# A long convolution with two expert layers: the filter's second layer in two passes, with its stored half reloaded in place

## The chip, the cores and the metric

The program runs on one core of a Trainium2 chip. The core has five engines that work side by side, each through its own instructions in order: PE (matrix products), DVE, ACT and POOL (elementwise work), and SP, which here only issues DMAs. The metric is the device time of one execution in microseconds.

## The reference, cut to what matters

```python
h_mlp  = np.maximum(pos_emb @ w1, 0.0) @ w2          # the filter: (12480 x 64) -> (12480 x 128)
h_filt = h_mlp * np.exp(-0.01 * pos)[:, None]
u = x * v                                            # 12480 x 128
y = irfft(rfft(u, 2S) * rfft(h_filt, 2S))[:S]        # a long convolution per channel
x = x * y
# then two expert layers, 128 -> 2048 -> 128: a rational function P/Q, then a leaky relu
h = x @ w_in;   g = (a0 + a1*h + a2*h**2 + a3*h**3) / (1 + |b0|*|h| + |b1|*h**2)
x = g @ w_out
h = x @ w2_in;  out = np.maximum(0.01 * h, h) @ w2_out
```

x, v and the filter are float32; the expert weights come as float64 and are converted on the chip.

## The kernel before, in words

A sequence position is split as row times 128 plus column; the filter is needed for its first 82 rows only (NH), the input for 98 (NU). The 128 channels are two groups g of 64. The convolution is a two-stage Fourier transform by matrix products, done for one group of channels after the other.

The front comes first. SP loads the position embeddings, then x and v in 16 chunks (`load_u`, L471; each chunk is four DMAs of x and four of v). `make_u(c)` (L476) multiplies a chunk on POOL, lets SP load v of chunk c+4 into the freed buffer, adds and subtracts halves on DVE into `u`, and lets SP load x of chunk c+6. The filter's first layer runs on PE and ACT (`mlp_t`, `mlp_1`). Its second layer is the loop at L542: 16 turns of four products with both channel groups, each product 256 columns wide. ACT copies the first group's part into `hf` (L549), which lies in the work tile `wk`, and the second group's part into a small block (L554) in the still unused first half of `A`, and stores that block to `hsc` in device memory through its own DMA queue (L555). Eleven calls of `make_u` stand between the turns.

Then come four transforms `first(g, s, i)` (L635), each of 16 turns: the filter (s = 1) and the input (s = 0) of group 0, then the input and the filter of group 1. A turn is four products into a PSUM bank and its eviction into `A`, on ACT (L649 to L651), or, for the turns that the table `DCH` (L657) names, on DVE (L645 to L647). The filter's transform writes the first half of `A`, where the stored blocks lay. After the two transforms of group 0 the second stage runs for its 23 blocks (`second`, `inverse`; L680 to L732, with loads of `c_m` and stores of `bd` by SP). The second stage uses the first 7936 elements of each row of `wk`, which is where `hf` lay, so the filter of group 1 has to come back: after blocks 10, 12, 14 and 16 SP loads a quarter of `hsc` into the free half of `u` (`raw`, L775), and in the third transform POOL copies it, transposed, into `hf` (L781 to L784).

Two more things run in between. `feed(n)` takes n steps of the conversion of the expert weights: six DVE steps and two POOL operations for each of 16 pieces, with a load and a store by SP. After the fourth transform the second stage of group 1 follows, and then, for the rest of the time, the expert layers in the order that `plan()` computes.

The order on each engine is the order of the code. PSUM banks for the second layer, the transforms and the second stage come from one pool of three (`ps_b`).

Of the kernel before, what the change touches and what calls it, by code (L numbers as in the profile page):

```python
# [10 lines left out]
F32 = mybir.dt.float32  # L11
# [13 lines left out]
N2 = 128  # L25
# [280 lines left out]
def conv_moe_moe(ctx: ExitStack, tc: tile.TileContext, I, out, dbg=None):  # L306
# [15 lines left out]
    hsc = dram.tile([NH, N2 // 2, 2, DG], F32, name="hsc")  # L322
# [36 lines left out]
    with tc.manual_schedule():  # L359
# [57 lines left out]
        pos = cut(Aw, 0, [N2, FO])  # L417
        pw = cut(wk, 0, [N2 // 2, 2, FO])
# [119 lines left out]
        ps_b = fstack.enter_context(tc.tile_pool(name="ps_b", bufs=3, space=PSUM, reuse_waits="tile"))  # L538
# [3 lines left out]
        for c in range(0, 64, 4):  # L542
            hps = ps_b.tile([128, 4, 2, NG, DG], F32, tag="b", name=f"hps{c}")
            for i in range(4):
                pe.matmul(
                    hps[:NH, i].rearrange("p q g d -> p (q g d)"), rh[:, c + i], w2b.rearrange("p q d -> p (q d)"),
                    start=True, stop=True,
                )
            act.copy(  # L549
                hf.rearrange("p d (q j) -> p q d j", q=2)[:NH, :, :, c : c + 4],  # L550
                hps[:NH, :, :, 0].rearrange("p j q d -> p q d j"),
            )
            hs = cut(Aw, 128 * c, [4, 2, DG])[:NH]
            act.copy(hs, hps[:NH, :, :, 1])  # L554
            spread(act, hsc[:, c : c + 4], hs)  # L555
            if c < 44:
                uc += 1
                make_u(uc)
# [76 lines left out]
        def first(g, s, i):  # L635
            c = i * 4
            ap_ = ps_b.tile([128, 4, 256], F32, tag="b", name=f"ap{g}_{s}_{c}")
            for i_ in range(4):
                lhs = hf[:, c + i_] if s else u[:NU, g * DG + c + i_]
                pe.matmul(ap_[:, i_, : 2 * K1], lhs, f1t if s else f1, start=True, stop=True)  # L640
            a = ap_[:, :, : 2 * K1].rearrange("p d (r k) -> p r k d", r=2)
            dst = Ak[:, 1 - s, :, :, c : c + 4]
            if i in DCH[g, s]:
                for r in range(2):
                    dve.tensor_copy(out=dst[:64, r], in_=a[:64, r])  # L645
                dve.tensor_copy(out=dst[64:, 0], in_=a[64:, 1])
                dve.tensor_scalar(out=dst[64:, 1], in0=a[64:, 0], scalar1=-1.0, scalar2=None, op0=ALU.mult)  # L647
            else:
                act.copy(dst[:64], a[:64])  # L649
                act.copy(dst[64:, 0], a[64:, 1])  # L650
                act.mul(dst[64:, 1], a[64:, 0], -1.0)  # L651

        def kn_(b):
# [4 lines left out]
            (0, 1): (9, 12, 15), (0, 0): (2, 6, 10, 14), (1, 0): (2, 6, 10, 14), (1, 1): (2, 6, 10, 14),  # L658
# [6 lines left out]
        def second_stage(g):  # L665
# [8 lines left out]
            def second(b):  # L674
# [3 lines left out]
                xp = ps_b.tile([128, KB, 2, 2, DG], F32, tag="b", name=f"xp{g}_{b}")  # L678
# [23 lines left out]
            def inverse(b, ps=ps_s):  # L702
                kn = kn_(b)
                yt = yts.pop(b)
                gp = ps.tile([128, 4, KB, DG], F32, tag="s" if ps is ps_s else "b", name=f"gp{g}_{b}")
# [41 lines left out]
            for b in range(NB - 3, NB):  # L747
                inverse(b, ps_b if b < NB - 1 and g else ps_s)()
# [20 lines left out]
        raw = cut(uw, 0, [N2 // 2, 2, DG])[:NH]  # L769
        for b in range(NB):  # L770
            run(st, 1)
            feed(2)
            if b in (10, 12, 14, 16):
                j = (b - 10) * 8
                spread(sp, raw[:, j : j + 16], hsc[:, j : j + 16])  # L775
        for i in range(16):
# [3 lines left out]
            elif i < 7:  # L780
                j = (i - 3) * 16  # L781
                pool.tensor_copy(
                    out=hf.rearrange("p d (q j) -> p q d j", q=2)[:NH, :, :, j : j + 16],
                    in_=raw[:, j : j + 16].rearrange("p j q d -> p q d j"),  # L784
                )
# [333 lines left out]
```

## Time and profile before

| what | value |
|---|---|
| median of three runs | 1674.22 us (1672.68 to 1675.82) |
| profiled execution | 1674.48 us, its span 1672.7 us |
| PE busy | 1594.3 us (95%) |
| POOL busy | 1402.4 us (84%) |
| DVE busy | 1460.0 us (87%) |
| ACT busy | 1356.3 us (81%) |
| moved by DMA | 97.31 MB |

All times below count from the start of the span. The first transform's first matmul is at 62.30, the second transform's at 104.88, the second stage of group 0 begins at 132.94, the third transform at 215.77, the fourth at 253.88, and the second stage of group 1 at 275.82. A row of the timeline gives start, length, engine, line, operation, tiles and shapes, how many were merged, and in brackets how long the engine had been idle before it and what released it. A merged length runs from the first start to the last end.

### The profile page before, as it was taken

To read this page: it belongs to the slowest core of one execution; us is meant where nothing else is said; L and a number is where in the kernel's file an instruction comes from. 1 tells how busy PE (TensorE), PEld (TensorE's weight loads), DVE (VectorE), ACT (ScalarE), POOL (GpSimd) and SP (SyncE) were. 2 spreads that over 40 slices of the span, in tenths; PEclk is the share of its full clock that TensorE was granted. 3 is DMA by queue.
4 is the path that set the end of the run, shared out by engine and by line. 5 is a ranking of instruction groups with operands and counts; after the bars stand their busy time and mean duration, and the time that the engine had idled before them with its cause. 6 is when DMAs were issued, how large, how long until landed. Compare 5 with 4: busy or idle time off the path is not lost.

```text
span 1672.7 us, 21634 instructions
## 1 busy us (share of the span) xinstructions
PE 1594.3 (95%) x6440; PEld 1132.6 (68%) x6440; DVE 1460.0 (87%) x2413; ACT 1356.3 (81%) x2678; POOL 1402.4 (84%) x1191
## 2 busy tenths in 40 slices
PE   7858979978999999999999999999999999999998
PEld 4657868865666666666666666666666666666665
DVE  4487766768999999999999999999999999999991
ACT  4633356447999999999999999999999999999994
POOL 4545653758999999999999999999999999999992
PEclk9979989987999999999999999999999999999999
DMA  6745824761101101011101111101011100000000
GB/s 174 238 125 179 264 93 148 246 156 26 26 18 36 31 14 31 18 36 31 31 15 27 27 31 31 31 19 31 18 31 31 36 14 23 1 6 10 5 6 15
DMA packets 90247, 97.31 MB, mean 58 GB/s; under 512 B 53308, under 2 KB 58662, under 8 KB 89290
## 3 DMA queue, kind: packets, MB, share of 16 engines
q1 hardware_dynamic: 87610, 92.85, 19.2%
q10 hardware_dynamic: 2520, 3.09, 0.6%
q8 instruction: 51, 0.84, 0.2%
q14 instruction: 66, 0.54, 0.1%
HBM read 70.84 MB, written 25.07 MB: 57 GB/s over the span
## 4 chain that ended last, share of the span: by engine, by line
PE 77%; DVE 2%; POOL 2%; ACT 1%; issue 1%; DMA 0%; SPq 0%; ACTq 0%; POOLq 0%; DVEq 0%
PE o1p L988 19%; PE o2p L988 15%; PE h L494 11%; PE h L496 10%; PE h L495 10%; PE yP L943 3%; PE xp L680 2%; PE gp L708 2%; PE o2p L494 1%; PE o2p L496 1%; PE o2p L495 1%; POOL wk L1024 1%; PE oP L1065 1%; PE xP L935 1%; DVE v L1026 0%
## 5 line engine op out<-in xcount | busy, mean ns | idle before, releaser
L1024 POOL TENSOR_TENSOR wk<-wk 128x972 f32<-128x972 f32 (+2 forms) x208 | 469.5, 2257 | 23.6 <-DVE wk L1021 21.2
L988 PE MATMUL o1p<-g,wo 128*128 128x486 f32 (+2 forms) x832 | 406.3, 572 | 8.0 <-DVE g L1039 8.0
L1015 POOL TENSOR_SCALAR wk<-wk,pars 128x486 f32<-128x486 f32 (+2 forms) x416 | 313.1, 753 | 35.1 <-ACT wk L1007 34.0
L1026 DVE SCALAR_TENSOR_TENSOR v<-wk,absb,v 128x486 f32<-128x486 f32 (+2 forms) x416 | 297.9, 716 | 11.6 <-ACT v L1009 10.7
L1033 DVE SCALAR_TENSOR_TENSOR v<-v,r 128x486 f32<-128x486 f32 (+2 forms) x416 | 275.1, 661 | 31.0 <-ACT r L1031 28.2
L988 PE MATMUL o2p<-wk,wo 128*128 128x486 f32 (+2 forms) x624 | 301.5, 566 | 0.0
L1009 ACT ACTIVATE v<-h,absb 128x486 f32<-128x486 f32 (+2 forms) x416 | 267.2, 645 | 14.1 <-DVE g L1039 10.5
L1021 DVE TENSOR_TENSOR wk<-h,wk 128x486 f32<-128x486 f32 (+2 forms) x416 | 271.9, 654 | 0.5 <-POOL wk L1015 0.2
L1036 DVE SCALAR_TENSOR_TENSOR v<-v,r 128x486 f32<-128x486 f32 (+2 forms) x416 | 267.2, 662 | 4.6
L1007 ACT ACTIVATE wk<-h 128x486 f32<-128x486 f32 (+2 forms) x416 | 239.8, 577 | 34.3 <-PE h L496 28.4
L1029 ACT ACTIVATE rho<-v 128x486 f32<-128x486 f32 (+2 forms) x416 | 241.2, 580 | 24.1 <-DVE v L1026 23.4
L1031 ACT ACTIVATE r<-rho 128x486 f32<-128x486 f32 (+2 forms) x416 | 255.7, 615 | 3.7
L1039 DVE TENSOR_TENSOR g<-wk,v 128x486 f32<-128x486 f32 (+2 forms) x416 | 254.0, 650 | 4.4 <-POOL wk L1024 3.0
L494 PE MATMUL h<-zh,wh 128*128 128x486 f32 (+2 forms) x416 | 253.9, 610 | 3.0 <-DVE wk L1021 2.0
L1046 ACT ACTIVATE wk<-h 128x486 f32<-128x486 f32 (+2 forms) x416 | 241.8, 581 | 12.4 <-PE h L496 11.7
L1017 POOL TENSOR_SCALAR wk<-wk,pars 128x972 f32<-128x972 f32 (+2 forms) x208 | 239.0, 1150 | 0.0
L988 PEld LDWEIGHTS o2p<-wk,wo 128*128 128x128 f32 x624 | 117.8, 189 | 109.9 <-issue 104.8
L494 PE MATMUL h<-uh,wh 128*128 128x486 f32 (+2 forms) x416 | 187.8, 451 | 0.9 <-ACT wk L1046 0.9
L988 PEld LDWEIGHTS o1p<-g,wo 128*128 128x128 f32 x832 | 155.2, 191 | 48.9 <-issue 15.7
L496 PE MATMUL h<-zh,wl 128*128 128x486 f32 (+2 forms) x416 | 159.8, 384 | 0.0
L495 PE MATMUL h<-zl,wh 128*128 128x486 f32 (+2 forms) x416 | 159.7, 384 | 0.0
L496 PE MATMUL h<-uh,wl 128*128 128x486 f32 (+2 forms) x416 | 158.9, 382 | 0.0
(106 smaller groups left out, 2566.1 us busy)
## 6 DMA issues: line engine op xcount, KB each, us to landing
bd<-wk SPq DMA_DIRECT2D x44, 256.0 KB
bt<-bd SPq DMA_DIRECT2D x100, 112.5 KB
wk<-c_m SPq DMA_DIRECT2D x43, 256.0 KB
dt<-c_d SPq DMA_DIRECT2D x25, 344.5 KB
A<-x SPq DMA_DIRECT2D x32, 192.0 KB
wk<-v SPq DMA_DIRECT2D x32, 192.0 KB
out<-ot SPq DMA_DIRECT2D x32, 192.0 KB
xc<-x SPq DMA_DIRECT2D x25, 240.0 KB
```

What stands on the lines that cost most here:

```text
L494: pe.matmul(dst, w_h, z_h, start=start, stop=False)
L495: pe.matmul(dst, w_h, z_l, start=False, stop=False)
L496: pe.matmul(dst, w_l, z_h, start=False, stop=stop)
L988: pe.matmul(o, wo[l][:, f], T.pop((src, n))[:, :w], start=(f == 0), stop=(f == NF - 1))
L1009: act.activation(bank("v", n)[:, :w], one("h1"), AF.Abs, scale=kk)
L1015: pool.tensor_scalar(out=q, in0=sq, scalar1=a3, scalar2=a1, op0=ALU.mult, op1=ALU.add)
L1021: dve.tensor_tensor(out=half("nn"), in0=one("h1"), in1=two("q"), op=ALU.mult)
L1024: pool.tensor_tensor(out=nn, in0=nn, in1=T["p", n][:, : 2 * w], op=ALU.add)
L1026: dve.scalar_tensor_tensor(out=one("v"), in0=two("s"), scalar=bb, in1=one("v"), op0=ALU.mult, op1=ALU.add)
L1031: act.activation(mk("r0"), one("rho"), AF.Square)
L1033: dve.scalar_tensor_tensor(out=one("v"), in0=one("v"), scalar=C1, in1=one("r0"), op0=ALU.add, op1=ALU.mult)
L1036: dve.scalar_tensor_tensor(out=one("v"), in0=one("v"), scalar=-2.0, in1=one("r0"), op0=ALU.add, op1=ALU.mult)
```

## The change

The second layer runs twice over its columns, once for each group, with products half as wide (128 columns) and eight of them in a turn. The first pass makes group 1 and evicts it into one block `ht` (82 rows of 64 x 128, in the layout of `hf`) in the first half of `A`; the second makes group 0 into `hf`. Between the passes SP, whose queue also carries the loads of x and v, stores `ht` to `hsc` in four pieces of 16 channels (each a DMA of 80 rows and one of 2). `hsc` has the layout of `hf`, so in the third transform, at turn 3, SP loads the four pieces straight into `hf`; the loads into `raw` and POOL's four copies are gone. The three banks of `ps_b` are now three named tiles taken in strict rotation (`bank_b`). The first transform has no eviction on DVE any more. Three of the eleven `make_u` stand in the first pass, eight in the second.

```diff
-    hsc = dram.tile([NH, N2 // 2, 2, DG], F32, name="hsc")
+    hsc = dram.tile([NH, DG, N2], F32, name="hsc")
...
+        ht = cut(Aw, 0, [DG, N2])
...
-        ps_b = fstack.enter_context(tc.tile_pool(name="ps_b", bufs=3, space=PSUM, reuse_waits="tile"))
+        ps_b = fstack.enter_context(tc.tile_pool(name="ps_b", bufs=1, space=PSUM, reuse_waits="tile"))
...
-        for c in range(0, 64, 4):
-            hps = ps_b.tile([128, 4, 2, NG, DG], F32, tag="b", name=f"hps{c}")
-            for i in range(4):
-                pe.matmul(
-                    hps[:NH, i].rearrange("p q g d -> p (q g d)"), rh[:, c + i], w2b.rearrange("p q d -> p (q d)"),
-                    start=True, stop=True,
+        turn_b = [0]
+
+        def bank_b(dims, name):
+
+            turn_b[0] += 1
+            return ps_b.tile([128, *dims], F32, tag=f"b{turn_b[0] % 3}", name=name)
+
+        for g, t in ((1, ht), (0, hf)):
+            for c in range(0, 64, 8):
+                hps = bank_b([8, 2, DG], f"hps{g}_{c}")
+                for i in range(8):
+                    pe.matmul(
+                        hps[:NH, i], rh[:, c + i], w2b[:, :, g * DG : (g + 1) * DG], start=True, stop=True
+                    )
+                act.copy(
+                    t.rearrange("p d (q j) -> p q d j", q=2)[:NH, :, :, c : c + 8],
+                    hps[:NH].rearrange("p j q d -> p q d j"),
                 )
-            act.copy(
-                hf.rearrange("p d (q j) -> p q d j", q=2)[:NH, :, :, c : c + 4],
-                hps[:NH, :, :, 0].rearrange("p j q d -> p q d j"),
-            )
-            hs = cut(Aw, 128 * c, [4, 2, DG])[:NH]
-            act.copy(hs, hps[:NH, :, :, 1])
-            spread(act, hsc[:, c : c + 4], hs)
-            if c < 44:
-                uc += 1
-                make_u(uc)
+                if c < 24 or not g:
+                    uc += 1
+                    make_u(uc)
+            if g:
+                for c in range(0, DG, 16):
+                    spread(sp, hsc[:, c : c + 16], ht[:NH, c : c + 16])
...
-            (0, 1): (9, 12, 15), (0, 0): (2, 6, 10, 14), (1, 0): (2, 6, 10, 14), (1, 1): (2, 6, 10, 14),
+            (0, 1): (), (0, 0): (2, 6, 10, 14), (1, 0): (2, 6, 10, 14), (1, 1): (2, 6, 10, 14),
...
-        raw = cut(uw, 0, [N2 // 2, 2, DG])[:NH]
         for b in range(NB):
             run(st, 1)
             feed(2)
-            if b in (10, 12, 14, 16):
-                j = (b - 10) * 8
-                spread(sp, raw[:, j : j + 16], hsc[:, j : j + 16])
         for i in range(16):
             first(1, 0, i)
             if i < 3:
                 run(st, 1)
-            elif i < 7:
-                j = (i - 3) * 16
-                pool.tensor_copy(
-                    out=hf.rearrange("p d (q j) -> p q d j", q=2)[:NH, :, :, j : j + 16],
-                    in_=raw[:, j : j + 16].rearrange("p j q d -> p q d j"),
-                )
+            elif i == 3:
+                for c in range(0, DG, 16):
+                    spread(sp, hf[:NH, c : c + 16], hsc[:, c : c + 16])
             if i >= 3:
                 feed(1)
```

First place, SP while the second layer runs. `A<-x` and `wk<-v` are the loads of the input, `hsc<-A` the store. A wait on DMAHWn is on one of eight completion names that all DMAs of SP and ACT share in turn. Before, the queue holds loads alone (ACT issues the stores):

```order
L355 DMA A<-x 96x512 [waits DMAHW1_49]
L355 DMA A<-x 2x512 [waits DMAHW2_49]
L355 DMA A<-x 96x512 [waits DMAHW4_49]
L355 DMA A<-x 1x512 [waits DMAHW6_49]
L355 DMA wk<-v 96x512 [waits DMAHW7_49]
L355 DMA wk<-v 2x512 [waits DMAHW1_49]
```

Now, after 16 further groups of such loads, the eight stores stand in it:

```order
L355 DMA A<-x 1x512 [waits DMAHW0_49]
L334 DMA hsc<-A 80x2048 [waits DMAHW1_49,Activation_49]
L336 DMA hsc<-A 2x2048 [waits DMAHW2_49]
L334 DMA hsc<-A 80x2048 [waits DMAHW3_49]
L336 DMA hsc<-A 2x2048 [waits DMAHW4_49]
L334 DMA hsc<-A 80x2048 [waits DMAHW5_49]
L336 DMA hsc<-A 2x2048 [waits DMAHW6_49]
L334 DMA hsc<-A 80x2048 [waits DMAHW7_49]
L336 DMA hsc<-A 2x2048 [waits DMAHW0_49]
L355 DMA wk<-v 96x512 [waits DMAHW1_49,Pool_49]
```

The names skipped before (a 3, then a 5) were taken by ACT's stores; now they go round by ones. Ten groups of loads follow the stores.

Second place, DVE from the last chunks of `u` to the second transform. L591 to L606 are conversion steps, `ap_1` the evictions of the first transform, `ap_0` those of the second. Before:

```order
L602 SCALAR_TENSOR_TENSOR wk<-wk 128x512
L645 COPY A<-ap_1_36_663 64x90x4 x2
L646 COPY A<-ap_1_36_663 64x90x4
L647 TENSOR_SCALAR A<-ap_1_36_663 64x90x4
L606 SCALAR_TENSOR_TENSOR wk<-wk 128x512
L591 TENSOR_SCALAR wk<-wk 128x512
L593 TENSOR_SCALAR wk<-wk 128x512
L645 COPY A<-ap_1_48_695 64x90x4 x2
```

Now (L599 to L614 are the same conversion steps):

```order
L604 TENSOR_SCALAR wk<-wk 128x512
L608 TENSOR_SCALAR wk<-wk 128x512
L610 SCALAR_TENSOR_TENSOR wk<-wk 128x512
L614 SCALAR_TENSOR_TENSOR wk<-wk 128x512
L599 TENSOR_SCALAR wk<-wk 128x512
L653 COPY A<-ap_0_8_775 64x90x4 x2
L654 COPY A<-ap_0_8_775 64x90x4
L655 TENSOR_SCALAR A<-ap_0_8_775 64x90x4
```

Three evictions of the first transform went; thirteen conversion steps now stand together ahead of the second transform's first eviction on DVE.

Third place, SP at the start of the third transform. `bd<-wk` are the last stores of the second stage, L587 and L631 the load and the store of the conversion. Now:

```order
L743 DMA bd<-wk 128x256 [waits DMAHW1_49,Activation_49]
L334 DMA wk<-hsc 80x2048 [waits DMAHW2_49,PE_49]
L336 DMA wk<-hsc 2x2048 [waits DMAHW3_49]
L334 DMA wk<-hsc 80x2048 [waits DMAHW4_49,DVE_49,Pool_49]
L336 DMA wk<-hsc 2x2048 [waits DMAHW5_49]
L334 DMA wk<-hsc 80x2048 [waits DMAHW6_49,PE_49]
L336 DMA wk<-hsc 2x2048 [waits DMAHW7_49]
L334 DMA wk<-hsc 80x2048 [waits DMAHW1_49,DMAHW0_49]
L336 DMA wk<-hsc 2x2048
L587 DMA wk<-moe_w_out 128x4x256 [waits DMAHW2_49,DVE_49]
L631 DMA wsc<-wk 128x512 [waits DMAHW3_49,Pool_49]
```

Before, the `bd` store was followed at once by the conversion's load; the eight loads from `hsc` stood earlier, among the blocks of the second stage.

## Rows read from the trace of the kernel before

**Rows 1.** the page, chain that ended last: shares of the span by engine, then by line

```profile
PE 77%; DVE 2%; POOL 2%; ACT 1%; issue 1%; DMA 0%; SPq 0%; ACTq 0%; POOLq 0%; DVEq 0%
PE o1p L988 19%; PE o2p L988 15%; PE h L494 11%; PE h L496 10%; PE h L495 10%; PE yP L943 3%; PE xp L680 2%; PE gp L708 2%; PE o2p L494 1%; PE o2p L496 1%; PE o2p L495 1%; POOL wk L1024 1%; PE oP L1065 1%; PE xP L935 1%; DVE v L1026 0%
```

**Rows 2.** the page, DMA line of the 40 slices (41.8 us each, busy tenths)

```profile
DMA  6745824761101101011101111101011100000000
```

**Rows 3.** busy time by stretch: PE, PEld, DVE, ACT, POOL; PE clock, DMA share, GB/s

```profile
28.00:36.00 8.00, 8.00 (x39) 5.56 (x38) 2.79 (x3) 4.44 (x9) 0.09 (x1) 1.00 0.31 88
...
70.00:80.00 10.00, 9.23 (x50) 7.58 (x51) 5.92 (x5) 9.78 (x19) 7.39 (x3) 1.00 0.85 255
...
91.00:105.00 14.00, 2.76 (x9) 2.29 (x9) 13.95 (x18) 0.00 (x0) 4.62 (x3) 0.50 0.29 93
...
184.00:196.00 12.00, 9.11 (x36) 7.52 (x35) 5.95 (x10) 2.27 (x5) 5.45 (x6) 0.86 1.03 306
```

**Rows 4.** waits of SP, 10 to 110 us: total, times, longest

```profile
SPq L355 <- DMA hsc<-A: 18.2, 11, 6.9
```

**Rows 5.** timeline of SP, groups of loads and the last stores

```profile
25.29 8.82 SPq L355 DMA_DIRECT2D wk<-v  x4
...
65.39 1.88 SPq L355 DMA_DIRECT2D wk<-v  x4
...
81.78 1.31 SPq L355 DMA_DIRECT2D wk<-v  x4
...
215.01 9.74 SPq L732 DMA_DIRECT2D bd<-wk  x5
```

**Rows 6.** timeline of PE, start of the second transform and of the second stage

```profile
104.88 2.77 PE L640 MATMUL ap<-f,u 98*128 98x180 f32 x8 [11.24 <-DVE A L647]
...
132.94 1.32 PE L680 MATMUL xp<-A,wk 128*128 128x256 f32 x5 [1.72 <-ACT A L651]
```

**Rows 7.** timeline of DVE, last chunks of u to the second transform

```profile
76.02 25.08 DVE L484 TENSOR_TENSOR u<-A 98x512 f32<-98x512 f32 x14 [2.12 <-POOL A L480]
...
100.94 0.41 DVE L591 TENSOR_SCALAR wk<-wk 128x512 int32<-128x512 int32 x1
...
102.87 0.95 DVE L645 COPY A<-ap 64x360 f32<-64x360 f32 x2
```

**Rows 8.** timeline of PE, second layer, and the short last block of the second stage

```profile
28.43 20.92 PE L545 MATMUL hps<-A 128*82 128x256 f32 x96
...
222.90 1.06 PE L712 MATMUL gp<-wk,em 128*128 128x128 f32 x8
```

**Rows 9.** timeline of ACT, first two turns of the first transform

```profile
66.76 0.75 ACT L649 COPY A<-ap 64x720 f32<-64x720 f32 x1 [4.03 <-DMA A<-x]
...
68.38 0.75 ACT L649 COPY A<-ap 64x720 f32<-64x720 f32 x1
```

**Rows 10.** timeline of PE and DVE, third and fourth transform

```profile
223.79 12.66 PE L640 MATMUL ap<-f,u 98*128 98x180 f32 x80
...
236.25 3.86 DVE L593 TENSOR_SCALAR wk<-wk 128x512 int32<-128x512 int32 x1 [5.41 <-POOL wk L613]
...
246.97 7.07 PE L640 MATMUL ap<-f,u 98*128 98x180 f32 x24 [10.52 <-DVE A L647]
...
253.88 20.27 PE L640 MATMUL ap<-f1t,wk 128*128 128x180 f32 x128
...
275.82 5.45 PE L680 MATMUL xp<-A,u 128*128 128x256 f32 x24 [1.68 <-ACT A L651]
```

**Rows 11.** timeline of PE and ACT, middle of the second stage

```profile
184.21 1.89 PE L680 MATMUL xp<-A,wk 128*128 128x256 f32 x8
...
188.27 0.59 ACT L725 COPY wk<-gp 128x512 f32<-128x512 f32 x1 [4.95 <-DMA bd<-wk]
...
189.00 3.44 PE L712 MATMUL gp<-wk,em 128*128 128x256 f32 x8 [2.90 <-ACT wk L725]
```

**Rows 12.** groups by line, POOL, 215 to 254 us: busy, mean ns | idle before, releaser

```profile
L782 POOL COPY wk<-u 82x2048 f32<-82x2048 f32 x4 | 15.1, 3803 | 10.2 <-DVE wk L606 10.2
```

More of the change, by code (lines that the diff above doesn't have):

```diff
@@ L636, in first @@
             c = i * 4
-            ap_ = ps_b.tile([128, 4, 256], F32, tag="b", name=f"ap{g}_{s}_{c}")
+            ap_ = bank_b([4, 256], f"ap{g}_{s}_{c}")
             for i_ in range(4):
@@ L677, in second @@
                 mt = mts.pop(b)
-                xp = ps_b.tile([128, KB, 2, 2, DG], F32, tag="b", name=f"xp{g}_{b}")
+                xp = bank_b([KB, 2, 2, DG], f"xp{g}_{b}")
                 for i in range(kn):
@@ L700, in second, with inverse @@
                     after()
-            def inverse(b, ps=ps_s):
+            def inverse(b, own=True):
                 kn = kn_(b)
                 yt = yts.pop(b)
-                gp = ps.tile([128, 4, KB, DG], F32, tag="s" if ps is ps_s else "b", name=f"gp{g}_{b}")
+                if own:
+                    gp = ps_s.tile([128, 4, KB, DG], F32, tag="s", name=f"gp{g}_{b}")
+                else:
+                    gp = bank_b([4, KB, DG], f"gp{g}_{b}")
                 if g:
@@ L747, in second_stage @@
             for b in range(NB - 3, NB):
-                inverse(b, ps_b if b < NB - 1 and g else ps_s)()
+                inverse(b, b == NB - 1 or not g)()
                 store()
```

## The prediction, made before the change was run

> **What bounds the kernel now.** I read the chain of waits first. Matrix work is 77% of it, nearly all in the expert layers of the last 1300 us [rows 1], and the edit touches no instruction there. What it can change lies in the first 276 us: filter, transforms and what feeds them. I read the slices next: the DMA digits are high only at the start [rows 2]. Third came the table by stretch, where three stand out [rows 3]. In 28 to 36 us the DMA engines move 88 GB/s, against 255 GB/s in 70 to 80 us. In 91 to 105 us PE does 2.76 us of work at half clock. In 184 to 196 us the DMA share is full and PE loses 3 us. Last I asked who waits there and between the transforms.
>
> The loading gap: SP loads x and v, and its longest named wait, 18.2 us in 11 pieces, is on stores of `hsc` [rows 4], which those loads never read. The order shows why: all DMAs of SP and ACT take turns on eight completion names (DMAHW0 to 7), and a DMA waits for the one that held its name before. So a load of x or v can stand behind a store that ACT issues after its next eviction. The four loads begun at 25.29 take 8.82 us to issue, where a group of four otherwise takes 1.31 [rows 5]. The end of the front stage: DVE is at work on `u` until 101.1, does five conversion steps, and only then evictions of the first transform; PE's second transform (group 0 of u) begins at 104.88, released by the last of them [rows 6, 7].
>
> **First part: the second layer and the first transform (to the start of block 0 of the second stage, now 132.94 [rows 6]).** Removed: 32 DMA issues on ACT, and with them the false waits of SP. Added: 64 more matmuls (128 more records and weight loads), half as wide; eight store DMAs of 2.69 MB in all (4 x 82 x 8 KB) on SP, between load groups. Moved: three DVE evictions to ACT. Each step:
>
> 1. Loads. A group of four goes out every 1.64 us ((81.78 - 65.39)/10 [rows 5]). The order puts 16 groups between the group at 25.29 and the stores: 25.29 + 17 x 1.64 = 53.2. SP then waits for nothing else, since pass one has ended (step 2). Behind the stores ten groups are queued, and POOL, DVE wait for those. The store at 255 to 306 GB/s [rows 3] is 10.5 to 8.8 us; I take 9.5, so the queue is free at 53.2 + 1.6 + 9.5 = 64.3 and the loads land by 64.3 + 16.4 = 80.7. DVE turns out a chunk of u in 3.58 us when POOL runs too (25.08/7 [rows 7]); six chunks are left behind the store, and before them one product on POOL of some 2.5 us. 64.3 + 2.5 + 21.5 = 88.3: u is ready then, not at 101.1.
> 2. PE. A record of 128 columns takes 1.06/8 = 0.13 us (the short last block [rows 8]). 256 of them are 34 us: from 28.43 to 62.4. Pass one ends near 45.5, before SP asks for it. ACT's copies of 1024 elements (some 1 us, between a 720-element one at 0.75 [rows 9] and twice a 512-element one) are under the 2.1 us of eight matmuls. `hf` is whole near 63.4, about where it is now.
> 3. First transform. Its output overwrites the place of the stored block, so the first eviction waits for the store, as now for the small ones (4.03 us, to 66.76 [rows 9]): 64.3 + 1 = 65.3. A turn on ACT is 1.62 us (68.38 - 66.76 [rows 9]). All 16 now: 25.9, to 91.2. So u (88.3) is no longer last, nor is DVE.
> 4. Second transform. The fourth has the same mix of evictions and takes 21.9 us (253.88 to 275.82 [rows 10]), to 113.1. Behind u stand on DVE now twelve conversion steps in a row (five took 1.9 us [rows 7]; twelve with two hand-overs to POOL some 8, an estimate), so the third turn's eviction comes near 97 to 99, and as the banks now turn strictly by three, the sixth turn waits for it: ACT, done with four turns at 97.7, loses about 2.8 us. That gives 115.9.
>
> Gain: 132.94 - 115.9 = 17.0. Bounds: 11.4, with the store at 255 GB/s (1 us more) and four turns of the first transform at the pace of PE at half clock, 2.77 for 1.62 (the row at 104.88 [rows 6]; PE waits for the store before them); 20.5, with the store at 306 GB/s and no hold in step 4.
>
> For step 2 the row says: eight records with 128-column weights and 128 columns streamed end 1.06 us after the first began, 0.13 each [rows 8]. From above a record is bounded by what one of twice the width takes now, 20.92/96 = 0.218. A rule of the Trainium skill speaks against 0.13: "TensorE: Matmul & The Clock Gate", section "The mechanism", says that a weight load overlaps running matmuls only when they use other row groups. The same page of the Trainium skill, section "LDWEIGHTS (loading the stationary operand)", gives columns / 1.2 ns, 68 ns for 82 columns, so in series with the matmul a record would take some 0.175 us, an estimate by that page, and the two passes 45 us instead of 34. The trace's 0.13 contradicts the serial reading.
>
> **Second part: the middle of the second stage.** Removed: four loads of 640 KB from `hsc` into u's space. At 188.27 ACT comes out of a 4.95 us wait for a `bd` store, PE stands idle 2.90 before 189.00, and the next eight records take 3.44 for 1.89 [rows 11]; DMA moves 306 GB/s with share 1.03 there [rows 3]. Without those loads the store lands in time: 2.9 + 1.55 = 4.5 us. Bounds 1.5 (only the slow records' share goes) and 6.
>
> **Third part: the third transform (group 1 of u).** Removed: four POOL copies, 15.1 us [rows 12]. While they run, DVE's conversion steps take 3.86 us and the first of them starts after 5.41 us of waiting for POOL; the eviction behind them holds PE for 10.52 us [rows 10]. Without them the turns from 223.79 on [rows 10] go at the pace of the fourth transform, 21.9/16 = 1.37: 13 x 1.37 = 17.8, so the fourth begins at 241.6 instead of 253.88: 12.3 us. Added: eight reload DMAs at the fourth turn, behind the last `bd` stores. SP issues those until 224.8 [rows 5], so the reload (2.69 MB, 8.8 to 10.5 us) is in place by about 236, five us before it is read. Behind it on SP stand a load of expert weights (0.5 MB) and a store. Landing near 238, the weights hold DVE by perhaps 2 us (its step is due near 236.5), inside what three banks cover. If the reload took 5 us more, the fourteenth to sixteenth turns would wait: 8 us left as the lower bound; 12.5 above, since the copies hide nothing else.
>
> **The sum.** 17.0 + 4.5 + 12.3 = 33.8. The profiled execution took 1674.48 (span 1672.7), 0.26 over the median of 1674.22. 1674.5 - 33.8 = 1640.7; I say 1641. All that follows (second stage of group 1, expert layers) has its order unchanged and is released by what is now earlier. Bounds: 11.4 + 1.5 + 8 = 20.9 gives 1653.6; 20.5 + 6 + 12.5 = 39 gives 1635.5.
>
> **The rivals.**
> - The store gives back the loading gain. For it: same bytes, same 16 engines, and the stores now stand in front of ten load groups, which DVE waits for. Then u comes near 98, the second transform starts about 7 us earlier than now instead of 13.7, and the front gives 10: 1648. Against it: the idle 28 to 36 us [rows 3] is used only if SP is free.
> - PE becomes the bound of the second layer: the weight load isn't hidden, and half as wide a record is no shorter than one now, 0.218. 256 of them are 55.8 us; hf is whole at 85.2, ACT's turns end at 112, the second transform at 134: the front loses 1, the time is 1659. Against it: [rows 8]. By the figures of that page of the Trainium skill it would be 1648.
> - It doesn't do what it says: other DMAs hold the eight names, so SP waits as long as before. The front gives only the moved evictions, some 4 us: 1654. Against it: no other engine than SP issues DMAs after ACT's 32 are gone.
> - Slower. One mechanism: the two big moves run at the rate of the quiet stretch, 88 GB/s [rows 3], and hold what is queued behind them on SP. 2.69 MB are then 30.6 us. In the front u and the first transform come 21 us later than I say (115.9 + 21 = 137); the reload ends near 256 and the weights behind it near 262, so the fourth transform starts 8 us later than now. 4 + 8 - 4.5 = 7.5 us lost: 1682. It decides from about 100 GB/s downward. Against it: the low rate is of a time when nothing was asked for.
>
> **How the numbers follow.** Forecast 0.67 (own range 1634 to 1647); store gives back 0.16; PE bound 0.05; not as it says 0.05; slower 0.03; the gains cancelled by a wait I don't see, no change, 0.04. The range 1634 to 1655 takes in both ends of the sum and the first rival, and leaves out about one in eight, mostly above. A measurement of this kernel tells 0.2% (3.3 us) from no change: faster 0.93, same 0.04, slower 0.03.
>
> **What would show it.** Right: no wait of SP on `hsc` among the loads before 50 us; a store of 2.69 MB between 53 and 65; u complete near 88 to 92; block 0 of the second stage near 116; no PE gap near the middle of the second stage; no POOL copy of 82x2048, and the fourth transform directly behind the third. Wrong: records of the second layer at 0.17 us or more; the first eviction of the first transform well after 68; DVE waiting for expert weights between the third and fourth transform; PE waiting for `hf`.

## The result, and the profile after

The changed kernel takes 1648.89 us (median of four runs, 1647.39 to 1650.82); the kernel before took 1673.76 beside it. The ratio is 0.984 [0.9824, 0.9855]. Forecast was 1641 with 1634 to 1655: faster as said and inside the range, but 24.9 us were gained of some 33, and the time lies just above the forecast's own 1634 to 1647.

The profiled executions (1647.39 with a span of 1645.6; before 1674.48 and 1672.7) show where. "Front" ends where PE starts block 0 of the second stage, "last part" begins at the first product of the expert layers.

| stretch, us | before | after | gained | forecast |
|---|---|---|---|---|
| front | 132.94 | 117.23 | 15.7 | 17.0 |
| second stage, group 0 | 82.83 | 78.09 | 4.7 | 4.5 |
| third and fourth transform | 60.05 | 51.35 | 8.7 | 12.3 |
| second stage, group 1 | 80.65 | 81.13 | -0.5 | 0 |
| last part | 1316.2 | 1317.8 | -1.6 | 0 |
| span | 1672.7 | 1645.6 | 27.1 | 33.8 |

SP in the front (start, us, queue, line, tile, count):

```profile
25.27 1.46 SPq L355 DMA_DIRECT2D wk<-v  x4
...
53.21 0.32 SPq L334 DMA_DIRECT2D hsc<-A  x1
...
61.21 3.33 SPq L355 DMA_DIRECT2D wk<-v  x4
```

The group at 25.27 goes out in 1.46 us where it took 8.82 [rows 5], and the stores begin at 53.21, as worked out. The rate of the quiet stretch [rows 3] has gone from 88 to 248 GB/s, and in 91 to 105 us PE now works (columns as in [rows 3]):

```profile
28.00:36.00 8.00, 8.00 (x67) 7.36 (x66) 6.90 (x3) 4.60 (x6) 6.39 (x3) 1.00 0.79 248
91.00:105.00 14.00, 11.46 (x63) 11.24 (x64) 10.99 (x24) 9.67 (x19) 4.54 (x4) 0.88 0.48 151
```

PE in the front (the second layer, then first and second transform, block 0, and a stall in the second stage), then ACT's first eviction of the first transform, then DVE (end of u, first conversion step, first eviction of the second transform):

```profile
29.17 28.11 PE L554 MATMUL hps<-A 128*82 128x128 f32 x256
...
68.69 20.85 PE L648 MATMUL ap<-f1t,wk 128*128 128x180 f32 x104 [6.38 <-ACT A L659]
92.36 8.02 PE L648 MATMUL ap<-f,u 98*128 98x180 f32 x40 [2.82 <-DVE wk L599]
101.56 13.95 PE L648 MATMUL ap<-f,u 98*128 98x180 f32 x88 [1.19 <-DVE A L655]
117.23 7.14 PE L688 MATMUL xp<-A,wk 128*128 128x256 f32 x32 [1.72 <-ACT A L659]
...
137.56 3.34 PE L723 MATMUL gp<-wk,em 128*128 128x256 f32 x8 [2.83 <-ACT wk L736]
```

```profile
67.05 0.75 ACT L657 COPY A<-ap 64x720 f32<-64x720 f32 x1 [8.72 <-DMA A<-x]
```

```profile
70.79 21.31 DVE L485 TENSOR_TENSOR u<-A 98x512 f32<-98x512 f32 x12 [8.18 <-POOL A L481]
91.96 0.40 DVE L599 TENSOR_SCALAR wk<-wk 128x512 int32<-128x512 int32 x1
...
99.47 0.95 DVE L653 COPY A<-ap 64x360 f32<-64x360 f32 x2
```

Read three things. 256 records take 28.11 us, 0.110 each. DVE stands 8.18 us without input just behind the store. And u is complete at 92.1 (70.79 and 21.31), while ACT does the last of its sixteen turns, so the second transform starts at 92.36 instead of 104.88 [rows 6], released by DVE after PE had stood for 2.82 us.

PE, DVE and SP from the third transform to the second stage of group 1 (answers to [rows 10]):

```profile
195.32 1.39 PE L648 MATMUL ap<-f,u 98*128 98x180 f32 x8
...
219.67 1.49 PE L648 MATMUL ap<-f1t,wk 128*128 128x180 f32 x8
224.48 20.51 PE L648 MATMUL ap<-f1t,wk 128*128 128x180 f32 x120 [3.32 <-DVE A L655]
246.67 5.45 PE L688 MATMUL xp<-A,u 128*128 128x256 f32 x24 [1.68 <-ACT A L659]
```

```profile
221.25 0.43 DVE L599 TENSOR_SCALAR wk<-wk 128x512 int32<-128x512 int32 x1 [4.97 <-DMA wk<-moe_w_out]
```

```profile
204.58 0.38 SPq L334 DMA_DIRECT2D wk<-hsc  x1
...
207.19 0.28 SPq L336 DMA_DIRECT2D wk<-hsc  x1
209.64 0.40 SPq L587 DMA_DIRECT2D wk<-moe_w_out  x1
```

The third transform runs through without a gap, but now the fourth is torn: one turn after its start PE waits 3.32 us for an eviction on DVE, and DVE had waited 4.97 us for expert weights. Their load was issued at 209.64, behind the eight DMAs of the reload. Two more readings bear on it: the waits of SP in 203 to 213 us, and what moved from the first DMA of the reload until the weights were there (columns as in [rows 3]):

```profile
SPq L587 <- DMA wk<-hsc: 4.2, 2, 2.1
```

```profile
204.60:221.20 16.60, 16.52 (x105) 15.68 (x103) 8.30 (x17) 15.68 (x30) 4.19 (x4) 1.00 0.99 246
```

SP itself was held for 2.1 us ahead of that load by a DMA of the reload, whose completion name the load takes over (DMAHW2 in the third order listing), and the DMA engines were full.

### The profile page after: what moved, and what is told of

Same layout as the page of the kernel before. It is cut to its first block, busy times and chain, and to the rows that moved or that the text cites. A ratio compares the mean times of both kernels' runs of the same rounds, so it can differ in the third digit from the quotient of the medians.

```text
span 1645.6 us, 21850 instructions
## 1 busy us (share of the span) xinstructions
PE 1588.4 (97%) x6568; PEld 1138.0 (69%) x6568; DVE 1459.0 (89%) x2401; ACT 1360.2 (83%) x2671; POOL 1391.5 (85%) x1187
## 4 chain that ended last, share of the span: by engine, by line
PE 86%; DMA 5%; DVE 3%; POOL 2%; SPq 1%; issue 1%; ACT 1%; ACTq 0%; DVEq 0%; POOLq 0%
PE o1p L992 20%; PE o2p L992 15%; PE h L495 11%; PE h L497 11%; PE h L496 11%; PE xp L688 4%; PE yP L947 4%; PE gp L723 2%; PE ap L648 2%; PE gp L719 2%; DMA A<-x 1%; PE o2p L495 1%; PE o2p L497 1%; PE o2p L496 1%; DMA wk<-v 1%
```

## The experiments

The table gives the milestones of every profile: start of the second transform, start of the second stage of group 0, its length, third and fourth transform together, last part.

| kernel | 2nd tr. | stage | length | 3rd+4th | last part | ratio to before |
|---|---|---|---|---|---|---|
| before | 104.88 | 132.94 | 82.8 | 60.1 | 1316.2 | 1 |
| after | 92.36 | 117.23 | 78.1 | 51.4 | 1317.8 | 0.984 [0.9824, 0.9855] |
| e1 | 91.32 | 116.17 | 78.0 | 46.1 | 1322.2 | 0.9813 [0.9792, 0.9835] |
| e2 | 91.19 | 116.06 | 81.7 | 46.2 | 1316.4 | 0.9824 [0.9804, 0.9844] |
| e3 | 104.10 | 125.80 | 82.7 | 58.9 | 1321.8 | 0.9971 [0.9956, 0.9987] |
| e4 | 101.13 | 125.59 | 83.7 | 59.5 | 1317.6 | 0.9968 [0.9955, 0.9981] |
| e5 | 94.21 | 119.08 | 80.1 | 59.7 | 1322.3 | 0.9906 [0.9888, 0.9925] |
| e6 | 94.24 | 118.98 | 78.8 | 47.4 | 1320.0 | 0.9799 [0.9778, 0.982] |
| e7 | 93.80 | 118.67 | 78.5 | 46.1 | 1318.0 | 0.9789 [0.9768, 0.981] |
| e8 | 93.89 | 121.86 | 77.0 | 49.9 | 1313.7 | 0.9786 [0.9762, 0.981] |
| e9 | 92.51 | 117.36 | 77.5 | 52.5 | 1320.4 | 0.9845 [0.9829, 0.986] |
| e10 | 90.60 | 115.55 | 74.9 | 47.0 | 1319.6 | 0.98 [0.9779, 0.982] |
| e11 | 95.26 | 117.09 | 77.0 | 47.5 | 1315.2 | 0.9778 [0.9758, 0.9798] |

e1 to e4, e5 to e8 and e9 to e11 ran on a chip each; of the same instructions the second transform began 2.6 us later on the second chip (e8 against e1), so fronts are compared within a group. One profile stands behind each row, and the same instructions do not always take the same time: up to the expert layers e8 has e1's, and yet it took 27.97 us from the second transform to the second stage (24.85 in e1) and 49.9 for 3rd+4th. In e8 PE stopped for 2.86 us before 103.09, and in 104 to 108 us the granted clock was 0.50. A difference of some 3 us between two rows therefore counts only where other rows bear it out.

**e1_spread_reload.**

```diff
-            elif i == 3:
-                for c in range(0, DG, 16):
-                    spread(sp, hf[:NH, c : c + 16], hsc[:, c : c + 16])
+            if i in (3, 6, 9, 12):
+                c = (i - 3) // 3 * 16
+                spread(sp, hf[:NH, c : c + 16], hsc[:, c : c + 16])
```

> The changed kernel with the four pieces of the reload issued at turns 3, 6, 9 and 12 of the third transform instead of all at turn 3; nothing else differs. Theory A (the load of expert weights stands behind 2.69 MB of reload on the same DMA engines, so DVE waits 4.97 us at 221.25 and PE 3.32 us at 224.48): that wait of DVE falls below 1 us, the fourth transform takes 21.9 us as it did before, so that the second stage of group 1 begins about 241.6 instead of 246.67, and the time falls by 5 us, to 1644 from 1648.9. Theory B (DVE's conversion is late there by itself, and the reload has nothing to do with it): the stall stays, 246 to 247, time 1648 to 1650.

The weights' load now goes out behind the first piece, and the fourth transform follows without a gap. SP, then PE:

```profile
204.16 0.40 SPq L587 DMA_DIRECT2D wk<-moe_w_out  x1
```

```profile
218.48 20.08 PE L648 MATMUL ap<-f1t,wk 128*128 128x180 f32 x128
240.23 5.45 PE L688 MATMUL xp<-A,u 128*128 128x256 f32 x24 [1.68 <-ACT A L659]
```

46.1 us instead of 51.4: theory A. Where the reload stands in one block it was 51.4 and 52.5 (after, e9), and with the pieces spread 46.1 to 49.9 in six profiles (e1, e6, e7, e8, e10, e11). The span fell by only 2.3, since the last part took 4.4 more (see e8).

**e2_reload_by_copies.** The changed kernel, but the block goes through u's space and POOL, in contiguous copies:

```diff
+        raw = cut(uw, 0, [DG, N2])[:NH]
...
+            if b in (10, 12, 14, 16):
+                j = (b - 10) * 8
+                spread(sp, raw[:, j : j + 16], hsc[:, j : j + 16])
...
+            elif i < 7:
+                j = (i - 3) * 16
+                pool.tensor_copy(out=hf[:NH, j : j + 16], in_=raw[:, j : j + 16])
```

> The changed kernel with its third part undone: the block is loaded into u's space during the second stage and POOL copies it into place in four copies, as before (the copies read a contiguous block now). Theory: the front stays (second stage at 117.2); a PE stall of about 3 us at a gp product comes back some 52 us into the second stage, which then takes 82 instead of 78.1 us; the third and fourth transform take about 60 instead of 51.4 us, unless the contiguous copies are shorter than the 3.8 us of before. Time 1648.9 + 4.5 + 8.7 = 1662. Rival (the raw loads have no part in the stall, it came from the place of a store of converted weights): second stage stays at 78, time 1657.5. Rival (the two expert waits of POOL don't hold DVE): time 1653.

The second stage lost 3.6 us again, in several small stalls. But the time was 1646.1, not the 1662 expected, for the transforms took 46.2 us with four copies beside them: I was wrong that the copies cost 8.7 us as such. PE, and two copies on POOL at 1.86 us (3.80 in [rows 12]):

```profile
197.77 1.39 PE L648 MATMUL ap<-f,u 98*128 98x180 f32 x8
...
222.17 20.07 PE L648 MATMUL ap<-f1t,wk 128*128 128x180 f32 x128
243.92 5.45 PE L688 MATMUL xp<-A,u 128*128 128x256 f32 x24 [1.68 <-ACT A L659]
```

```profile
210.20 3.72 POOL L793 COPY wk<-u 82x2048 f32<-82x2048 f32 x2
```

**e5_strided_copies.** e2 with the copies of before:

```diff
-                pool.tensor_copy(out=hf[:NH, j : j + 16], in_=raw[:, j : j + 16])
+                pool.tensor_copy(
+                    out=hf.rearrange("p d (q j) -> p q d j", q=2)[:NH, :, :, j : j + 16],
+                    in_=cut(uw, 0, [N2 // 2, 2, DG])[:NH, j : j + 16].rearrange("p j q d -> p q d j"),
+                )
```

> e2_reload_by_copies with one thing changed: POOL's four copies read and write in the order of the kernel before (16 neighbouring words written, each read 512 bytes after the last) instead of contiguous blocks; the same bytes and the same four copies. The values of group 1's filter come out permuted, so the output is not the reference's; no instruction is added or left out. Theory (it was the stride of the copies that held the third transform, not that they exist): each copy takes 3.8 us instead of 1.9, DVE's conversion step beside it waits or stretches, PE stalls some 10 us on an eviction of DVE, and third and fourth transform together take 58 to 61 us instead of 46.2; time 1646.1 + 13 = 1659. Rival (the copies were harmless, the third transform of before was held by DVE's or SP's order): 46 to 49 us, time 1646 to 1649.

59.7 us: the whole loss is back. POOL, DVE, PE:

```profile
209.90 7.66 POOL L793 COPY wk<-u 82x2048 f32<-82x2048 f32 x2 [10.17 <-DVE wk L614]
...
219.55 7.45 POOL L793 COPY wk<-u 82x2048 f32<-82x2048 f32 x2
```

```profile
219.64 3.86 DVE L601 TENSOR_SCALAR wk<-wk 128x512 int32<-128x512 int32 x1 [5.42 <-POOL wk L621]
```

```profile
230.36 6.70 PE L648 MATMUL ap<-f,u 98*128 98x180 f32 x24 [10.52 <-DVE A L655]
...
258.84 5.45 PE L688 MATMUL xp<-A,u 128*128 128x256 f32 x24 [1.68 <-ACT A L659]
```

A copy takes 3.83 us (3.73 in the second pair), a conversion step of DVE (0.42 alone) 3.86 beside it, and PE stands 10.52 us, to the hundredth as in [rows 10]. So it was the stride; whether that of the reading or of the writing, no run separates. In the Trainium skill's "SBUF — State Buffer", section "SBUF: two separate sides", POOL and DVE (in its two-port modes, or with two inputs in SBUF) share a pair of ports that one of them holds for its whole instruction. The trace agrees so far as the step on DVE ends with the copy on POOL; ports it does not show.

**e3_one_pass_sp_stores and e4_evictions_moved.** Each takes one piece of the front's change into the kernel before:

```diff
-            spread(act, hsc[:, c : c + 4], hs)
+            if c % 16 == 12:
+                spread(sp, hsc[:, c - 12 : c + 4], cut(Aw, 128 * (c - 12), [16, 2, DG])[:NH])
```

> The kernel before with one thing changed: group 1's half is stored by SP in four pieces of 16 columns, each behind the turn that completes it, instead of by ACT after every turn; one pass, DVE's three evictions, raw loads and copies as before. Theory (the second pass is what lets the store go early): the gap of SP's loads at 25 to 36 us goes, and u is complete near 92, but the last piece is complete only when the pass ends, near 60, and stands behind all loads on SP, so the first transform waits for it until 80 or later; second stage at 128 to 134 instead of 132.94; time 1669 to 1675. Rival (the queue of the stores is the whole of the front's gain): second stage near 118 to 120, time 1660.

SP, ACT and PE of e3:

```profile
25.36 1.34 SPq L355 DMA_DIRECT2D wk<-v  x4
```

```profile
82.39 0.75 ACT L650 COPY A<-ap 64x720 f32<-64x720 f32 x1 [24.73 <-DMA hsc<-A]
```

```profile
104.10 19.98 PE L641 MATMUL ap<-f,u 98*128 98x180 f32 x128
125.80 7.14 PE L681 MATMUL xp<-A,wk 128*128 128x256 f32 x32 [1.72 <-ACT A L652]
```

The loading gap is gone by the queue alone, and u is complete at 86.1. But the last piece stands behind all loads; ACT's first eviction waits 24.73 us for it. The second stage came at 125.80, better than the 128 I gave at least, since with u early nothing held the second transform (21.7 us). The rival's 118 to 120 is refuted: the second pass is what gets the whole store out early, its last large piece at 58.77 instead of 75.23.

```diff
-            (0, 1): (9, 12, 15), (0, 0): (2, 6, 10, 14),
+            (0, 1): (), (0, 0): (2, 6, 10, 14),
```

> The kernel before with only the three evictions of the first transform moved from DVE to ACT. By the working of the prediction the second transform begins when u is complete, at 101.1 instead of 104.88, and loses up to 2.8 us to the conversion steps that now stand ahead of its first eviction on DVE: second stage at 129 to 132 instead of 132.94, time 1670 to 1673. Rival (the evictions on DVE are what holds the front): second stage below 125, time below 1666. Rival (nothing moves): 1673.8.

```profile
101.13 8.30 PE L640 MATMUL ap<-f,u 98*128 98x180 f32 x40 [12.50 <-DVE wk L591]
...
125.59 8.83 PE L680 MATMUL xp<-A,wk 128*128 128x256 f32 x32 [1.72 <-ACT A L651]
```

PE starts at 101.13, as u is complete, exactly as said, but the front ends at 125.59, outside the 129 to 132 expected: 7.35 us won, not the 4 that my rival "not as it says" put on it. The transform itself took 24.46 us, for 28.06 in the kernel before, where after its first turn PE stopped 1.98 us more for DVE and the granted clock stayed at 0.50 until 113 us; in e4 it was back at 105.

**e6_no_hold, e7_early_store.** The hold is DVE's late first eviction in the second transform (99.47 in the kernel after), for which PE stops 1.19 us. The two kernels are e1, with the steps of conversion moved out of the first transform, and with the store cut in two and begun two chunks earlier:

```diff
-            if i >= 4:
+            if i >= 10:
                 feed(1)
...
-            if i % 4:
-                feed(1)
+            feed(1)
```

> e1_spread_reload with six of the twelve conversion steps taken away from the first transform (they begin at its turn 10 instead of 4) and four more given in the second transform. Theory (step 4: DVE's first eviction of the second transform stands behind twelve conversion steps and holds PE): DVE is free about 95, PE runs the second transform without the hold, 22.0 to 22.6 us instead of 24.85 from its start to the second stage; second stage at 113.5 instead of 116.2, all later parts as much earlier; time 1641.4 against 1644.1. Rival (ACT's evictions set the pace there anyway): second stage at 115.5 to 116.2, time 1643.5 to 1644.

```profile
94.24 22.89 PE L648 MATMUL ap<-f,u 98*128 98x180 f32 x128 [4.20 <-DVE wk L599]
118.98 7.14 PE L688 MATMUL xp<-A,wk 128*128 128x256 f32 x32 [1.84 <-ACT A L659]
```

```profile
96.00:98.00 2.00, 2.00 (x9) 2.00 (x8) 1.18 (x2) 0.93 (x2) 1.90 (x2) 0.50 0.53 135
100.00:102.00 2.00, 2.00 (x14) 2.00 (x14) 0.92 (x2) 0.99 (x3) 0.00 (x0) 1.00 0.48 138
```

PE no longer stops, and yet 24.74 us. The windows show why: it comes out of 4.20 us of waiting for u at 0.50 of the clock, and the first turns crawl. In the changed kernel the clock was back by 96 us and the hold came behind. The time, 1644.65, shows nothing of the 2.7 us expected either.

```diff
+                if not g and c < 16:
+                    for k in range(4 * c, 4 * c + 32, 16):
+                        spread(sp, hsc[:, k : k + 16], ht[:NH, k : k + 16])
+                for _ in range(c < 8 if g else 1 + (c in (32, 56))):
```

> e1_spread_reload with the store of ht begun two chunks of u earlier on SP and cut in two: two pieces behind 13 groups of loads, one chunk's loads, then two pieces. Theory (the one block of store is what keeps DVE 8.2 us without u and ACT 8.7 us from its first eviction): the store is issued at 46 to 56, the first eviction comes at 61 to 63 instead of 66 to 67, DVE's gap halves, the second transform begins at 88 to 90 instead of 91.3 and the second stage at 113 to 115; time 1641 to 1643. Rival (the loads bind, whatever the order): u still at 91 to 92, second stage at 116, time 1644.

ACT, DVE:

```profile
63.91 0.75 ACT L657 COPY A<-ap 64x720 f32<-64x720 f32 x1 [5.31 <-DMA wk<-v]
```

```profile
68.21 1.94 DVE L485 TENSOR_TENSOR u<-A 98x512 f32<-98x512 f32 x2 [7.10 <-POOL A L481]
...
93.39 0.41 DVE L599 TENSOR_SCALAR wk<-wk 128x512 int32<-128x512 int32 x1
```

ACT starts earlier (63.91), but DVE still stands 7.10 us without input (and 3.58 before), and u is complete at 93.4, as in e8 with the store in one block (93.5): the rival. Moving half of the store ahead of some loads did not make u earlier, and the first transform was not the last to end.

**e8_pe_kept_busy.** e1, with this ahead of the first product of the expert stage:

```diff
+            for _ in range(0 if j else 36):
+                pe.matmul(t[:, :128], ident, ident, start=True, stop=True)
```

> e1_spread_reload with 36 extra products of ident by ident (128x128) on PE in the gap before the first product of the expert stage; their results are overwritten. Theory (the 1 to 6 us by which the part behind the first expert product differs between kernels with the same instructions there is TensorE's clock: it falls to half in that 4.5 us gap and comes back 10 us later in the one profile, 23 to 27 us later in the other): the clock stays at or near full from there on, and that part takes 1310 to 1315 us, against 1322.2 in the profile of e1 and 1316.2 to 1317.8 in those before and after; time 1636 to 1640. Rival (the expert stage starts as slowly for want of its inputs, and the clock matters little): 1316 to 1322, time 1643 to 1646.

The granted clock (third column from the right) in the kernel after, 5 to 8 us behind the first expert product; in the kernel before, 6 to 9 us behind it; and in e8, within the gap and just behind that product's start at 331.58:

```profile
333.00:336.00 3.00, 3.00 (x15) 3.00 (x15) 3.00 (x9) 1.59 (x4) 1.10 (x2) 0.50 0.02 5
```

```profile
362.00:365.00 3.00, 2.68 (x23) 2.45 (x22) 3.00 (x9) 2.63 (x7) 2.50 (x3) 1.00 0.65 183
```

```profile
322.00:326.00 4.00, 4.00 (x39) 4.00 (x38) 0.00 (x0) 0.00 (x0) 0.00 (x0) 1.00 0.32 112
332.00:336.00 4.00, 2.93 (x22) 2.69 (x23) 2.44 (x7) 3.52 (x11) 2.63 (x5) 1.00 1.09 220
```

In all ten profiles without filling products PE's clock falls to half in the 4.5 us gap ahead of the expert layers. It was back 3 us behind the first expert product in before and e2 (last part 1316.2 and 1316.4), and 16 to 19 us behind it in the other eight (1317.6 to 1322.3, 1320.0 in the mean). Among these eight it matters whether the clock falls once more. The stretch 36 to 44 us behind the product, in after and in e1:

```profile
364.00:372.00 8.00, 7.54 (x40) 5.43 (x39) 7.48 (x18) 6.53 (x16) 7.59 (x8) 1.00 0.00 0
```

```profile
357.00:365.00 8.00, 7.80 (x28) 6.96 (x29) 4.96 (x13) 3.46 (x8) 5.36 (x6) 0.50 0.00 0
```

In after, e4 and e7 it stays at 1.00 there, and their last parts are the shortest of the eight (1317.6 to 1318.0); in the other five it falls. Counted from the first expert product, the last xP product (the transpose of x) stands at 71.8 us in e2, 73.2 in after and 77.7 in e1 (at 396.94, 400.96 and 398.79): the differences that the last parts end with (1316.4, 1317.8, 1322.2) are there by then. So they arise where the clock differs, and the changed kernel itself has been seen both ways (1317.8 in after, 1320.4 in e9).

With the filling the clock stays at 1.00 across the gap, and the last part takes 1313.7. The filling itself made the stage before it 1.8 us longer. For the whole kernel no gain is shown: the median of 1642.24 lies between the theory's 1640 and the rival's 1643, and the ratio of 0.9786 is that of e7 without filling (0.9789).

**e9_changed_again, e10_store_later_pe_busy, e11_all.** e10 is e1 with 28 filling products and the conversion's store three steps later; e11 adds e6's edit and 24 filling products ahead of the second transform.

```diff
+                    if n == 3 and st:
+                        sp.dma_start(*st)
+                        st = None
...
+            for _ in range(24 if (g, s, i) == (0, 0, 0) else 0):
+                pe.matmul(ap_[:, 0, :128], ident, ident, start=True, stop=True)
```

> The changed kernel as it is, a second time, beside the next two on one chip. If the milestones of its first profile are its own and not of one chip: second stage of group 0 at 117 to 119.5, 77.5 to 79 us long; DVE again waits 4 to 6 us for expert weights behind the reload, PE 2.5 to 4 us; third and fourth transform 50.5 to 52 us; ratio to the kernel before 0.982 to 0.986. The part behind the first expert product between 1316 and 1323 us, by when the clock returns.

> e1_spread_reload with two further edits: the store of the converted weights goes out three conversion steps later on SP (so that the bd stores of the first blocks no longer stand behind it), and 28 extra products of ident by ident in the gap before the expert stage. Theory: the one PE stall left in the second stage (2.8 us at a gp product about 20 us into it, then eight products at half clock, 1.5 us) goes, the stage takes 73.5 to 75 us instead of 78; third and fourth transform 46.2; the part behind the first expert product 1311 to 1315 us; ratio 0.975 to 0.978. Rival for the stall (it is the first blocks' own depth of two buffers, whatever stands on SP): stage 77 to 79 us.

> e10 with two edits at the front: the conversion steps begin at turn 10 of the first transform as in e6_no_hold, and 24 extra products of ident by ident stand before the second transform, where PE waits for u. e6 took the hold away and got nothing, since PE came out of its wait at half clock and the first three turns were slow (24.74 us to the second stage). Theory (hold and clock each keep the second transform at about 24.8, and only both together give it back): 21.9 to 22.6 us from its start to the second stage, 2.3 to 2.9 us less than e10; ratio 0.973 to 0.977. Rival (something else sets that pace): 24 to 25 us, same time as e10.

e9 repeated the changed kernel's milestones; its 3rd+4th is half a us over what I gave. In e10 the second stage took 74.9 us: the stall still left (PE at 137.56 above) came from a `bd` store behind the converted weights' store on SP. After its filling PE still stood 1.85 us for x (before 319.46), the clock fell, and the last part took 1319.6, not the 1311 to 1315 expected; in e11, with the same 28 products, that wait was 1.36 us and the clock stayed at 1.00 (1315.2). PE of e11 (the filling is the 48 records at 89.80):

```profile
89.80 5.62 PE L655 MATMUL ap<-ident 128*128 128x128 f32 x48
95.26 19.99 PE L658 MATMUL ap<-f,u 98*128 98x180 f32 x128
117.09 8.83 PE L698 MATMUL xp<-A,wk 128*128 128x256 f32 x32 [1.84 <-ACT A L669]
```

From its start the second transform takes 21.83 us, for 24.95 in e10: hold and clock, only both together, give 3 us back (e3, with neither, has 21.70). But behind the 24 products it began 2.6 us after u was complete (92.66), which ate the gain. e11 has the lowest ratio of all, 0.9778 [0.9758, 0.9798], against 0.9845 [0.9829, 0.986] for the changed kernel on the same chip; it lies just above the 0.973 to 0.977 expected and is not clear of e10's 0.98 [0.9779, 0.982], which missed its 0.975 to 0.978 too.

## Why the prediction was right, and where it was not

**Direction and mechanism.** The gap of the loads came from the shared completion names: with ACT's stores gone SP never waits on one before 50 us, in after, e3 and e7 alike; with them it does (8.69 us in e4). All three stretches gained, in the order foretold.

The time is also that of the first rival, by which the store gives back the loading gain (1648), but it was not reached in that rival's way: u came at 92.1 and not near 98, and the front gave 15.7 us and not 10. And one of the prediction's own signs of being wrong did appear: DVE waited for expert weights between the third and the fourth transform.

**Step 1, too small by 3.8 us.** u came at 92.1, not 88.3. The store's start was exact (53.2); I gave the loads ahead of it 1.6 us and the store 9.5, end 64.3. The sum let POOL's next product begin at 64.3; it began at 68.41. Of these 4.1 us, 1.6 are a group's loads behind the store, which the sum left out, and 2.5 the store. At the 254 to 271 GB/s moved there (45 to 55 and 55 to 65 us), the 13.8 us from 53.2 to ACT's first eviction carry some 3.6 MB: the block and 0.9 MB of loads (an estimate). The other order of e7 did not help u.

**Step 2, right, with reserve.** 0.110 us per record, under the 0.13 taken [rows 8] and far from the rival's 0.218. The weight loads go on beside the products: in 28 to 36 us PE is busy for all 8.00 us (67 records) and the loads for 7.36 (66). So the estimate of 0.175, which puts the two in series by a rule of the Trainium skill's "TensorE: Matmul & The Clock Gate", section "The mechanism", does not hold here, where each record has new weights in the same rows; that section also lets a load go ahead into a background weight buffer, and no run tells whether this is such a case.

**Step 3, the times right within 2 us, the conclusion not.** First eviction 67.05 for 65.3, ACT's last near 92.8 for 91.2. But "u (88.3) is no longer last" failed with step 1: PE stood 2.82 us for u. Since ACT had been put down as the last, at 91.2, a u that came 3.8 us late cost the front only 1.3.

**Step 4, the size right and the reason half.** 24.87 us for 24.7. The hold is real (1.19 us, eviction at 99.47), but taking it away gave nothing: the wait for u before it costs clock, which I had not counted. e11 shows both.

**Second part, right.** 4.7 for 4.5, and PE's stall at 189.00 [rows 11] is gone. With the raw loads back a stall returns 55 us into the stage, and 3.6 us (e2) and 2.0 us (e5) with it; that all of the 4.7 is theirs is not shown.

**Third part, the step that failed.** "Landing near 238, the weights hold DVE by perhaps 2 us (...), inside what three banks cover": they held it 4.97, and PE 3.32. Counted from the start of the third transform, DVE asked when it was said to (at 216.3), but the weights landed 3.7 us later than said, 11.6 us after their load's issue and 16.6 after the reload's. The 246 GB/s of that stretch are some 4.1 MB (an estimate), where the sum counted 3.2: a further load of weights (212.82) and a store went beside them. And the sum had put at nothing the 2.1 us that SP waited for the reload's completion name, the mechanism of the front once more. The fourth transform took 27.0 us for 21.9; that the third went 1.5 us faster than said (16.3 for 17.8) hid a part of it. e1 recovers 5.3 us by moving the pieces apart, which ends both waits; with that the gain would have been 13.9, over the 12.3 forecast. And the cause I named was too wide: not POOL's copies, but their stride (e2, e5).

**"Unchanged" after 275.82, missed by 2.1 us.** 1.6 of it, a quarter of the shortfall, is in the last part, where the clock returned 17 us behind the first product instead of 3 and then did not fall a second time: 1316.2 to 1322.3 in the ten profiles whose instructions there are the same. What decides when the clock returns stays open.

The shortfall of 6.7 us of span is thus: front 1.3, third part 3.6, behind it 2.1, less 0.2.

## What to carry to other kernels

Ask of each big transfer what small one stands behind it on the same engines, and move the big one in pieces. Before a copy is removed, see whether making it contiguous is enough. And price every wait of PE twice: the wait, and the half clock behind it.

## Not expected of the hardware

POOL's 82x2048 copy takes 3.83 us strided and 1.86 contiguous, and a step on DVE beside the strided one took 3.86 us instead of 0.42. When the clock came back behind the expert gap, and whether it fell once more, moved the last part by up to 6 us (1316.2 to 1322.3), more than most edits here. Taking away a hold of PE gained nothing while the clock was half (e6), and 3 us once it was full (e11).
